# A head's keys in one DMA with runs of 64 KB, into two overlapping homes in turn: cached attention with a dense block, one core

## The chip, the cores and the metric

The kernel runs on one core of one Trainium2 chip. The metric is the device time of one execution in microseconds. Of the version before there are three runs: 1279.92 us in the median, 1279.47 the lowest and 1280.14 the highest. A profiled execution of the same kernel stands beside them, and the rows in this document come from its trace.

## What is computed

One token passes through a layer: layer norm, attention of 32 heads over a cache of 32768 keys and values per head, output projection, and a dense block with the Mish activation. Everything is bf16. Cut to what matters:

```python
H, Sk, Dh, D, F = 32, 32768, 128, 512, 1376
q = (layernorm(x) @ wq).reshape(1, 1, H, Dh)            # one query per head
scores = einsum("bhqd,bhkd->bhqk", q, k_cache) * Dh ** -0.5
o = einsum("bhqk,bhkd->bhqd", softmax(scores), v_cache)
h = x + o.reshape(1, 1, H * Dh) @ wo
a = layernorm(h) @ w1 + b1
out = h + (a * tanh(softplus(a))) @ w2
```

k_cache and v_cache hold 8 MiB per head each, 512 MiB in all; every byte of them is read once. The weights come to about 11.2 MB.

## The kernel before, in words

**Tiling.** A head's 32768 keys lie as 128 partitions of 256 rows, 128 numbers each (SCOLS = 256). A tile is 128 keys by 128 numbers: row r of every partition. The 256 tiles of a head go through TensorE in 32 groups of GT = 8.

**Storage.** One array in SBUF, `ring`, has six slots of 32 KB per partition (L214). Slots 0 and 1 are the home of the two halves of a head's keys, slots 2 and 3 of its values, slot 4 of wq and later of w1 and w2, slot 5 of wo (HOMES, L284). There is one home for keys and one for values, so the DMA of the next head's half waits until this head's half has been used (`freed_by`, L295).

**Queues.** All big DMAs are started by SP, in the order written at L279 to L282: wq; then for each head the first half of the keys, the second half, the values; then wo in three pieces, w1, w2 in two. SP takes them one after the other: before each it waits for what frees the place, then starts it (L330 to L355). A key DMA moves a run of 32 KB per partition, a value DMA one of 64 KB; the values of the last head come in two halves.

**The loop.** The 32 heads are a hardware loop on TensorE, VectorE and ScalarE (`rounds`, L86, and `one`, L504). The loop's counter is in a register of each engine; waits inside the loop compare a semaphore with a multiple of the counter (L84). The order on each engine is fixed when the program is written. A round does the following.

1. `k_group` (L442), 32 times: TensorE transposes 8 key tiles into one of four PSUM banks (L452); the first transpose of each half waits for that half's DMA. VectorE copies the bank to SBUF as bf16 (L455). Three groups later TensorE multiplies the 8 transposed tiles with the query, one column of scores each (`scores`, L429). The last transpose of a half frees the half's home.
2. `soft_max`, `soft_a`, `soft_b` (L477 to L491): the maximum over all scores, by VectorE over columns, TensorE over partitions, and back.
3. `soft_exp` (L493): ScalarE computes the exponential of all 256 columns in one instruction, which also sums them, and writes `pbuf`.
4. `pv` (L462): 256 products of a value tile with its column of `pbuf` (L466). The first waits for the exponential and for the values' DMA; the last frees the values' home. After 64 of them comes the sum over partitions (`soft_c`, L498), whose reciprocal VectorE takes (L501).
5. `oev` (L472): VectorE scales the result and puts it into column h of `oT`, at an address held in a register (L473).

**Around the loop.** Ahead of it are the layer norm and the 32 queries (L405). Behind it are the output projection (L538), the second layer norm and the dense block (L555 to L577), whose result goes out by a DMA from SP (L356). GpSimd has small work at the start: identity patterns, and 31 memsets of one number which only raise the semaphore of the last head's second half of values, so that the loop's waits hold in every round (L367).

Of the kernel before, what the change touches and what calls it, by code (L numbers as in the profile page):

```python
# [168 lines left out]
def build_kernel(nc, A_x, A_k_cache, A_v_cache, A_wq, A_wo, B_w1, B_b1, B_w2, out):  # L169
# [27 lines left out]
    assert W1 + (FJ + 1) * D <= SLOT  # L197
# [16 lines left out]
    ring = sb([128, NS, SLOT], BF16, "ring")  # L214
# [6 lines left out]
    esum = sb([128, 1], F32, "esum")  # L221
# [3 lines left out]
    skip = sb([1, H], F32, "skip")  # L225
# [17 lines left out]
    outr = sb([128, 128], BF16, "outr")  # L243
# [9 lines left out]
    C_REG = hlp[:, 129:130]  # L253
# [9 lines left out]
    kinds = [PE, ACT, DVE, POOL, SP, "exp", "pmax", "gmax", "qc", "A", "B", "C", "pv", "nb", "rcp"]  # L263
    kinds += [f"{k}{i}" for i in range(2 * GPS) for k in ("ev", "tr", "qk")]
    sems = {k: sem(f"s_{k}") for k in kinds}
    ready = [sem(f"ready{i}") for i in range(NS)]
# [17 lines left out]
    HOMES = {"k": 0, "v": HALVES, "wq": 2 * HALVES, "w1": 2 * HALVES, "w2": 2 * HALVES, "wo": 2 * HALVES + 1}  # L284

    def slot_of(what):
        return HOMES[what[0]] + (what[2] if what[0] == "k" else 0)

    def ready_wait(what):
        return (ready[slot_of(what)], 16 * (what[1] + 1 if what[0] in "kv" else 1))  # L290

    def free_name(what):
        return "free" + "_".join(map(str, what))

    def freed_by(what):  # L295
        if what[0] in ("w1", "w2"):
            return [free_name(WQ)]
# [4 lines left out]
    def flat_of(what):  # L302
        if what[0] == "v":
            return ring[:, HALVES:2 * HALVES, :].rearrange("p s x -> p (s x)")
        return ring[:, slot_of(what), :]

    def tiles_of(what):
        return flat_of(what).rearrange("p (r d) -> p r d", d=Dh)

    wq_v = ring[:, slot_of(("wq",)), :].rearrange("p (k n) -> p k n", k=KC)  # L310
    wo_f = ring[:, slot_of(("wo",)), :]
    wo_v = wo_f.rearrange("p (j n) -> p j n", j=32)
    w12 = ring[:, slot_of(("w1",)), :]
    w1_v = w12[:, 0:W1].rearrange("p (k n) -> p k n", k=KC)
    w2_v = w12[:, W1:W1 + (FJ + 1) * D].rearrange("p (j n) -> p j n", j=FJ + 1)

    events = {}

    def program(S):
# [10 lines left out]
        for what in order:  # L330
            slot = slot_of(what)
            S.wait(SP, freed_by(what))
            flat = flat_of(what)
            if what[0] == "wq":
                start(wq_v, A_wq.rearrange("(k p) n -> p k n", k=KC), ready[slot])
            elif what[0] == "wo":
                j0, j1 = WO_J[what[1]:what[1] + 2]
                start(wo_f[:, j0 * D:j1 * D], A_wo.rearrange("(p j) n -> p (j n)", j=32)[:, j0 * D:j1 * D], s_wo[what[1]])
            elif what[0] == "w1":
                start(w1_v, B_w1.rearrange("(k p) n -> p k n", k=KC), s_w1)  # L340
            elif what[0] == "w2":
                j0, j1 = W2_J[what[1]:what[1] + 2]
                if j0 < FJ:
                    start(w2_v[:, j0:j1, :], B_w2[j0 * 128:j1 * 128, :].rearrange("(j p) n -> p j n", p=128), s_w2[what[1]])
                else:
                    start(w2_v[0:FLAST, FJ, :], B_w2[FJ * 128:F, :], s_w2[what[1]])
            else:
                cache = A_k_cache if what[0] == "k" else A_v_cache
                rows = cache[0, what[1], :, :].rearrange("(p r) d -> p (r d)", r=SCOLS)
                at = what[2] * SLOT if what[0] == "k" else 0  # L350
                if what == ("v", H - 1):
                    start(flat[:, 0:SLOT], rows[:, 0:SLOT], ready[slot])
                    start(flat[:, SLOT:], rows[:, SLOT:], s_half)
                else:
                    start(flat, rows[:, at:at + flat.shape[-1]], ready[slot])  # L355
# [16 lines left out]
        S.dma(POOL, lambda: g.dma_start(b1r[FJ:FJ + 1, 0:FLAST], B_b1[FJ * 128:F].rearrange("(o p) -> o p", o=1)).then_inc(s_b1, 16))  # L372
        S.step(DVE, lambda: v.memset(oT[:, :], 0.0), name="oTz")
# [27 lines left out]
        for h in range(H):  # L401
            for kc in range(KC):
                last = h == H - 1 and kc == KC - 1
                bg = kc - NE if h == H - 1 else None
                S.step(PE, lambda h=h, kc=kc: t_.matmul(Q_REG[:, h:h + 1], wq_v[:, kc, h * Dh:(h + 1) * Dh],  # L405
                                                         xnT[:, 0, kc:kc + 1], start=(kc == 0), stop=(kc == KC - 1)),
                       name=([f"qkb{bg}"] + (["q", free_name(WQ)] if last else []) if bg is not None else None),
                       kind=(f"qk{bg % (2 * GPS)}" if bg is not None else None),
                       waits=(["xn0", ready_wait(("wq",))] if h == 0 and kc == 0 else ()))
# [27 lines left out]
        def k_group(h, half, gi):  # L437
            what = ("k", h, half)
            bg = count[0]
            count[0] += 1  # L440
            kt = tiles_of(what)
            tb = T_b[bg % NT]  # L442
            for r in range(GT):
                waits = []
                if r == 0:
                    if gi == 0:
                        waits.append(ready_wait(what))
# [4 lines left out]
                S.step(PE, lambda r=r: t_.matmul(tb[:, r * 128:(r + 1) * 128], kt[:, gi * GT + r, :], identb[:, :],  # L452
# [5 lines left out]
            pend.append((h, half * TPS + gi * GT, bg))  # L458
# [3 lines left out]
        def pv(h, r0, r1):  # L462
            vt = tiles_of(("v", h))
            for r in range(r0, r1):
                last = r == SCOLS - 1
                S.step(PE, lambda r=r, last=last: t_.matmul(o_ps[:, 0:1], vt[:, r, :], pbuf[:, r:r + 1],  # L466
                                                            start=(r == 0), stop=last),
                       name=([free_name(("v", h)), f"pv{h}"] if last else None), kind=("pv" if last else None),
                       waits=([f"exp{h}", ready_wait(("v", h))] if r == 0 else
# [23 lines left out]
        def soft_exp(h):  # L493
            S.step(ACT, lambda: a.activation(pbuf[:, :], S_ps[:, 0:SCOLS], ACTF.Exp,  # L494
                                             bias=nb[:, :], scale=SC, accum_out=esum[:, :]),
                   name=f"exp{h}", waits=[f"nb{h}"], kind="exp")

        def soft_c(h):  # L498
            S.step(PE, lambda: t_.matmul(C_REG, onesm[:, :], esum[:, :], start=True, stop=True),  # L499
                   name=f"C{h}", waits=[f"exp{h}"], kind="C")  # L500
            S.step(DVE, lambda: v.reciprocal(rtotc[:, :], C_REG), name=f"rcp{h}",  # L501
                   waits=[f"C{h}"], kind="rcp")

        def one(n):  # L504
            h = n - 1
            for half in range(HALVES):
                for gi in range(GPS):
                    k_group(h, half, gi)
# [112 lines left out]
```

## Time and profile before

| what | value |
|---|---|
| median of three runs | 1279.92 us |
| the profiled execution's own time | 1279.57 us |
| its span, first to last instruction | 1277.8 us |
| DMA read from HBM | 548.08 MB |
| mean rate over the span | 429 GB/s |
| mean granted TensorE clock | 0.768 of full |
| TensorE's matmuls, number | 25131 |

How to read it: the difference between the execution's time and its span lies before the first and after the last instruction. In the profile PE is TensorE's matmuls, PEld its weight loads (they overlap), DVE is VectorE, ACT ScalarE, POOL GpSimd, SP SyncE; a letter q behind an engine marks an instruction that its sequencer handles, such as a register operation or the start of a DMA. A row of the timeline has start, length, engine, line, operation and tiles, the number of equal instructions merged in it, and in brackets the idle time of the engine ahead of it with what ended it. The chain of waits is followed back from the last instruction, at each step to what released it. A view of one line gives the shortest, median and longest duration in ns, and the first and last start in us.

### The profile page before, as it was taken

Reading aid. Unit: us, or ns where it says so; the run is one execution under the profiler, and the core shown is the slowest. Engines: PE = TensorE matmul, PEld = TensorE weight load, DVE = VectorE, ACT = ScalarE, POOL = GpSimd, SP = SyncE. Lnnn points to the kernel's source line nnn. Section 1 sums busy time; section 2 is a strip of 40 time slices with the busy share of each in tenths; the row PEclk is TensorE's granted clock in tenths of the full one; section 3 lists DMA queues with packets and bytes.
Section 4 is the critical chain, followed back from the end, with each engine's and each line's share of the span. In section 5 each row is a group of like instructions: output and inputs, shape, how many; then the busy total and the mean of one; then the engine's idle time right before and its main releaser. Section 6 shows DMA issues by size and latency. Waiting matters only on the chain.

```text
span 1277.8 us, 53266 instructions
## 1 busy us (share of the span) xinstructions
PE 1013.8 (79%) x25131; PEld 992.0 (78%) x25131; DVE 715.1 (56%) x1247; ACT 20.6 (2%) x70; POOL 3.3 (0%) x40
## 2 busy tenths in 40 slices
PE   3789877879777889777888778797778797778886
PEld 3789877878777878777888778787778797778885
DVE  2566544566444666445665445664446664456652
ACT  0000000000000000000000000000000000000000
POOL 1000000000000000000000000000000000000000
PEclk9788776888677887767887768886778877678875
DMA  9999999999999999999999999999999999999998
GB/s 407 426 425 436 443 427 421 439 428 446 433 431 425 432 430 449 427 423 436 429 444 435 429 426 432 429 451 427 431 427 430 429 450 427 427 432 430 451 418 328
DMA packets 16955, 548.25 MB, mean 429 GB/s; under 512 B 1744, under 2 KB 3120, under 8 KB 3760
## 3 DMA queue, kind: packets, MB, share of 16 engines
q1 hardware_dynamic: 16872, 548.09, 99.6%
q8 instruction: 9, 0.15, 0.0%
q0 software_dynamic: 64, 0.00, 0.0%
q14 instruction: 2, 0.02, 0.0%
q10 hardware_dynamic: 8, 0.00, 0.0%
HBM read 548.08 MB, written 0.00 MB: 429 GB/s over the span
## 4 chain that ended last, share of the span: by engine, by line
DMA 76%; PE 22%; issue 1%; DVE 0%; SPq 0%; ACT 0%; ACTq 0%
DMA ring<-in_A_v_cache_dram 71%; PE ops L466 17%; DMA ring<-in_B_w_dram 4%; PE tps L452 3%; DMA ring<-in_A_k_cache_dram 2%; PE hlp L499 1%; PE sps L429 1%; SPq L328 0%; DVE ering L455 0%; PE tps L571 0%; PE hlp L484 0%; PE hlp L489 0%; DVE pmax L478 0%; DVE gmax L486 0%; ACT pbuf L494 0%
## 5 line engine op out<-in xcount | busy, mean ns | idle before, releaser
L455 DVE COPY ering<-tps 128x1024 bf16<-128x1024 bf16 x1024 | 669.6, 692 | 125.3 <-PE tps L452 124.6
L452 PE MATMUL tps<-identb,ring 128*128 128x128 bf16 x8192 | 670.8, 233 | 74.5 <-DMA ring<-in_A_k_cache_dram 72.0
L452 PEld LDWEIGHTS tps<-identb,ring 128*128 128x128 bf16 x8192 | 524.1, 104 | 77.3 <-DMA ring<-in_A_k_cache_dram 74.5
L429 PE MATMUL sps<-qcur,ering 128*128 128x1 bf16 x8192 | 343.9, 164 | 8.7 <-DVE ering L455 6.7
L466 PEld LDWEIGHTS ops<-pbuf,ring 128*128 128x128 bf16 x8192 | 229.7, 105 | 132.1 <-issue 129.3
L466 PE MATMUL ops<-pbuf,ring 128*128 128x1 bf16 x8192 | 227.7, 165 | 130.1 <-DMA ring<-in_A_v_cache_dram 123.6
L429 PEld LDWEIGHTS sps<-qcur,ering 128*128 128x128 bf16 x8192 | 310.4, 97 | 11.6 <-DVE ering L455 9.4
L501 DVE RECIPROCAL rtotc<-hlp 128x1 f32<-128x1 f32 x32 | 5.4, 168 | 193.9 <-PE hlp L499 193.9
L473 DVE TENSOR_TENSOR oT<-ops,rtotc 128x1 f32 x32 | 5.2, 161 | 166.2 <-PE ops L466 166.2
L494 ACT ACTIVATE pbuf<-sps,nbias 128x256 bf16<-128x256 f32 x32 | 15.2, 474 | 1229.5 <-DVE nbias L491 1229.5
L489 PEld LDWEIGHTS hlp<-gmax,onesmat 1*128 1x128 f32 x64 | 11.7, 227 | 21.6 <-DVE gmax L486 21.6
L484 PE MATMUL hlp<-ident,pmax 128*1 128x128 f32 x64 | 12.4, 276 | 16.6 <-DVE pmax L478 16.6
L489 PE MATMUL hlp<-gmax,onesmat 1*128 1x1 f32 x64 | 14.4, 292 | 11.9 <-DVE gmax L486 11.9
L478 DVE TENSOR_REDUCE pmax<-sps 128x1 f32<-128x256 f32 x32 | 13.6, 424 | 16.5 <-PE sps L429 16.5
L499 PE MATMUL hlp<-esum,onesmat 128*128 128x1 f32 x64 | 18.1, 352 | 0.0
L484 PEld LDWEIGHTS hlp<-ident,pmax 128*1 128x1 f32 x64 | 2.7, 81 | 19.4 <-DVE pmax L478 19.4
L486 DVE TENSOR_REDUCE gmax<-hlp 1x1 f32<-1x128 f32 x32 | 8.9, 279 | 13.4 <-PE hlp L484 13.4
L499 PEld LDWEIGHTS hlp<-esum,onesmat 128*128 128x128 f32 x64 | 16.1, 312 | 0.0
L491 DVE TENSOR_SCALAR nbias<-hlp 128x1 f32<-128x1 f32 x32 | 5.0, 158 | 17.4 <-PE hlp L489 17.4
L405 PE MATMUL hlp<-xnT,ring 128*128 128x1 bf16 x128 | 3.6, 165 | 9.7 <-DMA ring<-in_A_wq_dram 9.7
L405 PEld LDWEIGHTS hlp<-xnT,ring 128*128 128x128 bf16 x128 | 3.5, 104 | 9.8 <-issue 9.8
L411 DVE CAST qT<-hlp 128x32 bf16<-128x32 f32 x1 | 0.2, 191 | 12.0 <-PE hlp L405 12.0
(59 smaller groups left out, 39.6 us busy)
## 6 DMA issues: line engine op xcount, KB each, us to landing
ring<-in_A_k_cache_dram SPq DMA_DIRECT2D x64, 4096.0 KB, 26.7
ring<-in_A_v_cache_dram SPq DMA_DIRECT2D x2, 4096.0 KB, 26.3
ring<-in_A_wq_dram SPq DMA_DIRECT2D x1, 4096.0 KB, 12.5
ring<-in_A_wo_dram SPq DMA_DIRECT2D x1, 2048.0 KB, 35.3
ring<-in_A_wo_dram SPq DMA_DIRECT2D x1, 1536.0 KB, 38.6
ring<-in_B_w_dram SPq DMA_DIRECT2D x1, 1376.0 KB, 42.4
ring<-in_B_w_dram SPq DMA_DIRECT2D x1, 1280.0 KB, 46.8
ring<-in_A_wo_dram SPq DMA_DIRECT2D x1, 512.0 KB, 39.4
```

The lines of the kernel that those rows point to most:

```text
L405: S.step(PE, lambda h=h, kc=kc: t_.matmul(Q_REG[:, h:h + 1], wq_v[:, kc, h * Dh:(h + 1) * Dh], xnT[:, 0, kc:kc + 1], start=(kc == 0), stop ...
L429: S.step(PE, lambda r=r: t_.matmul(S_ps[:, col0 + r:col0 + r + 1], ering[:, bg % NE, r, :], qcur[:, :], start=True, stop=True), name=(name ...
L452: S.step(PE, lambda r=r: t_.matmul(tb[:, r * 128:(r + 1) * 128], kt[:, gi * GT + r, :], identb[:, :], is_transpose=True, start=True, stop= ...
L455: S.step(DVE, lambda: v.tensor_copy(ering[:, bg % NE, :, :].rearrange("p r d -> p (r d)"), tb[:, :]), name=f"ev{bg}", waits=[f"trb{bg}", f ...
L466: S.step(PE, lambda r=r, last=last: t_.matmul(o_ps[:, 0:1], vt[:, r, :], pbuf[:, r:r + 1], start=(r == 0), stop=last), name=([free_name((" ...
L478: S.step(DVE, lambda: v.tensor_reduce(pmax[:, :], S_ps[:, 0:SCOLS], AXX, ALU.max), name=f"pmax{h}", waits=[f"qkh{h}"], kind="pmax")
L484: S.step(PE, lambda: t_.matmul(A_REG, pmax[:, :], ident[:, :], start=True, stop=True), name=f"A{h}", waits=[f"pmax{h}", "ident"], kind="A")
L486: S.step(DVE, lambda: v.tensor_reduce(gmax[:, :], A_REG, AXX, ALU.max), name=f"gmax{h}", waits=[f"A{h}"], kind="gmax")
L489: S.step(PE, lambda: t_.matmul(B_REG, onesm[0:1, :], gmax[:, :], start=True, stop=True), name=f"B{h}", waits=[f"gmax{h}", "consts0"], kind ...
L494: S.step(ACT, lambda: a.activation(pbuf[:, :], S_ps[:, 0:SCOLS], ACTF.Exp, bias=nb[:, :], scale=SC, accum_out=esum[:, :]), name=f"exp{h}", ...
L499: S.step(PE, lambda: t_.matmul(C_REG, onesm[:, :], esum[:, :], start=True, stop=True), name=f"C{h}", waits=[f"exp{h}"], kind="C")
L501: S.step(DVE, lambda: v.reciprocal(rtotc[:, :], C_REG), name=f"rcp{h}", waits=[f"C{h}"], kind="rcp")
```

## The change

A head's keys come in one DMA, as its values do, with a run of 64 KB per partition. Two whole homes for keys don't fit, so two homes overlap: keys take 256 + 80 tiles' room, heads with an even number use the first 256, heads with an odd number the last 256. The 176 tiles in the middle belong to both homes; their place doesn't depend on the head. They are transposed first, as score columns 0 to 175. The other 80 lie in front of the middle for even heads and behind it for odd ones; they come as columns 176 to 255, and their address is computed from the loop's counter (`S.base`).

The next head's DMA is started when the last of the 176 tiles has been transposed (`free_k`). The score columns no longer stand in the order of the rows, so the exponential is done in two instructions, one per part, each written to the place in `pbuf` where the values' order wants it (a register address, too), and their two sums are added by one more instruction of VectorE (`etot`). In the instruction order of the changed kernel a fused register operation stands in front of each of the 80 transposes in TensorE's loop, and one in front of each exponential on ScalarE.

Heads 0, 30 and 31 get their keys in three DMAs, of 88, 88 and 80 columns. TensorE waits for each of the three parts in every round; for the heads between, 58 memsets of GpSimd, which wait for the first head's parts, raise the semaphores of parts 1 and 2. w1 gets a home of its own, w2 goes into the first 80 tiles of the keys' room, wo into wq's home. The output row uses part of `ering`.

The core of the diff:

```diff
+    DYN = 80
+    FIX = SCOLS - DYN
+    CUT = [0, FIX // 2, FIX, SCOLS]
+    KB, VB, WA, WB_ = (SCOLS + DYN) * Dh, SCOLS * Dh, SLOT, W1 + 640
...
+    PARTS = [0, H - 2, H - 1]
+    def parts(h):
+        return range(3) if h in PARTS else (None,)
     for h in range(H):
-        order += [("k", h, half) for half in range(HALVES)] + [("v", h)]
+        order += [("k", h, part) for part in parts(h)] + [("v", h)]
...
+        if what[0] == "wo":
+            return ["free_wq"]
+        if what[0] == "w2":
+            return [f"free_d{H - 2}"]
+        if what[0] == "k" and what[2] == 2 and what[1] > 0:
+            return [f"free_d{what[1] - 1}"]
         if what[0] in "kv" and what[1] > 0:
-            return [free_name((what[0], what[1] - 1) + what[2:])]
+            return [f"free_{what[0]}{what[1] - 1}"]
...
+    def base(h):
+        return DYN * (h % 2)
...
+                if what[0] == "k" and what[2] is None:
+                    start(k_f[:, base(h) * Dh:(base(h) + SCOLS) * Dh], rows, ready["k0"])
+                elif what[0] == "k":
+                    c0, c1 = CUT[what[2]:what[2] + 2]
+                    t0 = DYN + c0 if c0 < FIX else (base(h) + FIX if h % 2 else 0)
+                    t1 = t0 + c1 - c0
+                    start(k_f[:, t0 * Dh:t1 * Dh], rows[:, (t0 - base(h)) * Dh:(t1 - base(h)) * Dh], ready[f"k{what[2]}"])
...
+        S.wait(POOL, [(ready["k1"], 16), (ready["k2"], 16)])
+            for n in range(H - len(PARTS)):
+                g.memset(skip[:, H + n:H + n + 1], 0.0).then_inc(ready["k1"], 16)
+                g.memset(skip[:, 2 * H + n:2 * H + n + 1], 0.0).then_inc(ready["k2"], 16)
...
+            def tile(c):
+                if c < FIX:
+                    return k_t[:, DYN + c, :]
+                if c == FIX:
+                    S.base = nc.snap(((S.counter + 1) % 2) * (SCOLS * Dh), engines=[LOOPED[PE]], min_val=0, max_val=SCOLS * Dh)
+                return k_f[:, bass.ds(S.base + (c - FIX) * Dh, Dh)]
...
-                    names = [f"trb{bg}"] + ([free_name(what)] if gi == GPS - 1 else [])
-                S.step(PE, lambda r=r: t_.matmul(tb[:, r * 128:(r + 1) * 128], kt[:, gi * GT + r, :], identb[:, :],
+                    names = [f"trb{bg}"] + ([f"free_k{h}"] if col0 + GT == FIX else [f"free_d{h}"] if col0 + GT == SCOLS else [])
+                S.step(PE, lambda r=r: t_.matmul(tb[:, r * 128:(r + 1) * 128], tile(col0 + r), identb[:, :],
...
-            S.step(ACT, lambda: a.activation(pbuf[:, :], S_ps[:, 0:SCOLS], ACTF.Exp,
-                                             bias=nb[:, :], scale=SC, accum_out=esum[:, :]),
-                   name=f"exp{h}", waits=[f"nb{h}"], kind="exp")
+            def part(n, c0, c1, at):
+                return lambda: a.activation(pbuf[:, bass.ds(at(S.counter), c1 - c0)], S_ps[:, c0:c1], ACTF.Exp,
+                                            bias=nb[:, :], scale=SC, accum_out=esum[:, n:n + 1])
+            S.step(ACT, part(0, 0, FIX, lambda i: (i % 2) * DYN), name=f"expa{h}", waits=[f"nb{h}"], kind="expa")
+            S.step(ACT, part(1, FIX, SCOLS, lambda i: ((i + 1) % 2) * FIX), name=f"exp{h}", waits=[f"nb{h}"], kind="exp")
...
+            S.step(DVE, lambda: v.tensor_reduce(etot[:, :], C_REG, AXX, ALU.add), name=f"etot{h}", waits=[f"C{h}"], kind="etot")
```

More of the change, by code (lines that the diff above doesn't have):

```diff
@@ L242, in build_kernel @@
     actT = sb([128, FJ + 1], BF16, "actT")
[L243 removed]
+    outr = ering[:, 0, 0, :]
     S_ps = ps([128, 512], "sps")
@@ L262, in build_kernel @@
     sem = nc.alloc_semaphore
-    kinds = [PE, ACT, DVE, POOL, SP, "exp", "pmax", "gmax", "qc", "A", "B", "C", "pv", "nb", "rcp"]
+    kinds = [PE, ACT, DVE, POOL, SP, "exp", "pmax", "gmax", "qc", "A", "B", "C", "pv", "nb", "rcp", "expa", "etot"]
     kinds += [f"{k}{i}" for i in range(2 * GPS) for k in ("ev", "tr", "qk")]
     sems = {k: sem(f"s_{k}") for k in kinds}
-    ready = [sem(f"ready{i}") for i in range(NS)]
+    ready = {k: sem(f"ready_{k}") for k in ("wq", "v", "k0", "k1", "k2")}
     s_x = sem("s_x")
```

94 lines of the change are left out of this document (40 added, 54 removed).

## The prediction

> **What bounds the kernel now.** I read the page first: engine shares, DMA rows, chain.
>
> ```profile
> span 1277.8 us, 53266 instructions
> PE 1013.8 (79%) x25131; PEld 992.0 (78%) x25131; DVE 715.1 (56%) x1247; ACT 20.6 (2%) x70; POOL 3.3 (0%) x40
> DMA  9999999999999999999999999999999999999998
> q1 hardware_dynamic: 16872, 548.09, 99.6%
> DMA 76%; PE 22%; issue 1%; DVE 0%; SPq 0%; ACT 0%; ACTq 0%
> ```
>
> The one hardware queue, which SP fills, keeps the 16 DMA engines busy for 99.6% of the span; TensorE is busy for 79%. Then the chain of waits in order of time, and the timeline of one head:
>
> ```profile
> 409.98 31.22 DMA ring<-in_A_v_cache_dram
> 441.34 1.84 PE ops L466 x64
> 448.76 31.23 DMA ring<-in_A_v_cache_dram
> ```
>
> ```profile
> 409.98 0.33 SPq L328 DMA_DIRECT2D ring<-in_A_v_cache_dram  x1
> 412.19 3.47 PE L452 MATMUL tps<-identb,ring 128*128 128x128 bf16 x32 [2.24 <-DMA ring<-in_A_k_cache_dram]
> 414.97 19.52 DVE L455 COPY ering<-tps 128x1024 bf16<-128x1024 bf16 x30 [0.16 <-PE tps L452]
> 415.50 0.34 PE L429 MATMUL sps<-qcur,ering 128*128 128x1 bf16 x8
> 416.32 0.45 PEld L452 LDWEIGHTS tps<-identb,ring 128*128 128x128 bf16 x8
> 423.45 10.67 SPq L328 DMA_DIRECT2D ring<-in_A_k_cache_dram  x2
> 436.98 0.47 ACT L494 ACTIVATE pbuf<-sps,nbias 128x256 bf16<-128x256 f32 x1 [37.92 <-DVE nbias L491]
> 437.35 0.19 ACT L494 ACTIVATION_READ_ACCUMULATOR pbuf<-sps,nbias 128x1 f32 x1
> 441.34 1.84 PE L466 MATMUL ops<-pbuf,ring 128*128 128x1 bf16 x64 [4.59 <-DMA ring<-in_A_v_cache_dram]
> 448.76 0.33 SPq L328 DMA_DIRECT2D ring<-in_A_v_cache_dram  x1
> 448.88 0.16 DVE L473 TENSOR_TENSOR oT<-ops,rtotc 128x1 f32 x1 [5.06 <-PE ops L466]
> 450.97 3.59 PE L452 MATMUL tps<-identb,ring 128*128 128x128 bf16 x32 [2.24 <-DMA ring<-in_A_k_cache_dram]
> ```
>
> The reader is to see a regular beat. Values are issued at 409.98 and 448.76: one head takes **38.78 us**. TensorE stands still twice in it, 4.59 us until the values land and 2.24 us until the next keys do, so the transfers set the beat. The chain's 31 us per value load are mostly queueing: the load was issued 11 us before the stream came to it. Landings of one head: first half of the keys at 412.1 (TensorE starts at 412.19), second about 9.7 us later (4.19 MB at the stream's 430 GB/s; 421.9), values at 441.2 (409.98 + 31.22).
>
> **The change, part by part.** Its own sum stands against the profiled execution: 1279.57 us, of which 1277.8 are the span and 1.8 lie around it; the median of the runs is 1279.92, 0.35 above. I add differences to the median.
>
> *Runs of 64 KB for keys.* The values already have them, so the trace prices them. Two DMA windows, the first nearly all values, the second nearly all keys:
>
> ```profile
> DMA packets 151, 8.09 MB, mean 418 GB/s; under 512 B 16, under 2 KB 16, under 8 KB 16
> q1 hardware_dynamic: 151, 8.09, 96.7%
> ...
> DMA packets 281, 8.68 MB, mean 446 GB/s; under 512 B 32, under 2 KB 32, under 8 KB 32
> q1 hardware_dynamic: 281, 8.68, 103.7%
> ```
>
> The windows are 19.35 and 19.45 us long. Bytes by busy time: 8.09 / (19.35 x 0.967) = 432.4 GB/s with 64 KB, 8.68 / (19.45 x 1.037) = 430.3 with 32 KB. A head's 8.39 MB of keys goes from 19.50 to 19.40 us: 0.095 us, and 29 heads (1 to 29) make 2.7 us. Heads 0, 30 and 31 come in three pieces of some 20 KB, 24 packets per engine instead of 16; at the same 0.095 us per 8 packets that gives back 0.3. The gain at most: **about 2.4 us** (1 to 3, as the rounded shares allow), if the stream stays unbroken. SP issues 29 key DMAs fewer at 0.33 us each; SP is idle most of the time, so nothing.
>
> *Keys in one piece: TensorE starts later.* Now a head's first transpose waits at 412.2 for half of the keys; afterwards it waits for all, at 421.9 in the same beat. The values land at 441.2 as before, so the 9.7 us come out of the slack behind. This is the heart of the sum, and I check both loads that wait on TensorE.
>
> (a) The next keys are issued after 176 tiles, 22 groups of 8. The groups' pace is 19.52 / 30 = 0.65 us; 16 groups ended at 423.45, 11.26 us after their start; 22 take 11.26 + 6 x 0.65 = 15.2. From 421.9 that is 437.1, while the values stream until 441.2. From issue to first bytes the start of the program shows:
>
> ```profile
> 0.75 0.46 SPq L328 DMA_DIRECT2D ring<-in_A_wq_dram  x1
> ...
> GB/s 0 0 0 0 0 0 0 0 0 0 0 0 0 0 0 0 0 0 0 0 0 0 7 7 0 765 546 437 0 0 0 0 0 0 109 109 0 109 437 655
> ```
>
> The slices of this window are 0.075 us: the bulk begins in the 26th, at 1.88, so 1.13 us after the issue. 437.1 + 1.1 = 438.2 is 3 us early. No stall.
>
> (b) The next values are issued when the products with the old ones end. In before they ended at 448.7, with 11 us to spare. Now: 421.9, plus key phase and softmax (412.19 to 437.55 and 0.1 to the first product: 25.45), plus 7.42 for the products (441.34 to 448.76), gives 454.8; plus 1.13 is 455.9, against 460.7 when the stream has ended the next keys (421.9 + 38.78). **Slack 4.8 us before anything is added to the phase.**
>
> *Register addresses: 80 per head, in the phase that has the slack.* The instruction order of the changed kernel has one fused register operation (three steps: add, multiply, add) in front of each of the 80 transposes, 10 groups. Before has one such operation per round on TensorE and two on VectorE:
>
> ```profile
> L91 PEldq FUSED_REGOPS  x32: 35/35/35, 21.0 to 1224.1; - x32
> L91 PEldq COMPARE_BRANCH  x33: 76/208/4558, 16.4 to 1259.2; - x33
> L84 PEldq EVENT_SEMAPHORE  x64: 51/51/51, 25.7 to 1251.1; - x64
> L84 DVEq EVENT_SEMAPHORE  x1056: 21/21/21, 17.4 to 1254.8; - x176
> L473 DVEq FUSED_REGOPS  x32: 57/57/71, 68.6 to 1259.8; - x32
> ```
>
> No row shows a register-addressed weight load. Lower bound: 35 ns, below the 56 ns that a transpose takes anyway (0.45 us for 8), nothing added. Upper bound: a sequencer operation as dear as the branch, 208 ns per tile. Nearest row: on VectorE the fused operation and its register-addressed instruction together. SP and VectorE were released by the same event; SP's DMA started at 448.76, L473's instruction at 448.88: 0.12 us for the pair. TensorE's sequencer spends 51 ns on a semaphore operation where VectorE's spends 21, so I add 0.03: **0.15 us per tile**. The 8 scores of a group (0.34 us with the pipeline's tail, 0.2 of issue: 0.65 - 0.45) are static and I set them behind: 8 x 0.15 + 0.2 = 1.40 instead of 0.65, 0.75 more; 10 groups: **X = 7.5 us per head**, between 0 and (8 x 0.208 + 0.2 - 0.65) x 10 = 12.
>
> The Trainium skill's TensorE: Matmul & The Clock Gate ("Wait — 56ns, not 53.3ns?") says that matmuls and weight loads normally go past the sequencer's microcode and that through it one costs about 62 ns; the 56 ns above agree with the first. An estimate by that page: 35 + 62 = 97 ns per tile, X = 3.3, no loss. No run here shows which way a register-addressed load takes.
>
> *Exponential in two.* One activation and one read of the sum (0.47 + 0.19) become two of each. Between 0.2 and 0.66 us more ahead of the products; two short ones overlap in part: 0.4. The added reduce on VectorE lies beside the three quarters of the products that follow. Nothing.
>
> *What else moves.* 58 GpSimd memsets wait for the first head's keys; nothing is queued behind them, and head 1's groups need them a beat later. Two more waits per head on TensorE for semaphores long reached: nothing (51 ns each if the cover is gone). Output and MLP weights have other homes, the same bytes and order. Nothing.
>
> *Sum.* First the clock, in rows by stretch (length; busy time of PE, PEld, DVE, ACT, POOL; granted clock; DMA share, GB/s): products, first 32 transposes, rest of the key phase.
>
> ```profile
> 402.50:409.90 7.40, 7.34 (x258) 7.34 (x258) 0.17 (x1) 0.00 (x0) 0.00 (x0) 0.50 0.99 425
> 412.19:415.44 3.25, 3.25 (x32) 3.25 (x32) 1.85 (x3) 0.00 (x0) 0.00 (x0) 0.51 1.08 464
> 415.44:437.60 22.16, 20.22 (x488) 19.66 (x485) 19.94 (x34) 0.56 (x2) 0.00 (x0) 0.96 1.02 439
> ```
>
> The first 32 transposes run at half clock (0.51) after the idle times. If TensorE hardly idles they take 4 x 0.45 = 1.8 instead of 3.25: 1.45 us back. The same page ("What's actually happening") puts the drop to half clock after about 3.4 us without work; the idle times of 4.59 and 2.24 and the 0.50 are in line with that.
>
> Keys landing, TensorE's turn, issue of the next values, their transfer and that of the keys behind them, landing: this ring goes around once in **two** heads, since the keys between are already on their way. Twice the beat = 0.05 + (25.45 - 1.45 + 0.4 + X) + 7.42 + 1.13 + 2 x 19.35 = 71.7 + X. It binds when it is over 2 x 38.7: at **X = 5.7**, that is 0.13 us per tile (4.3 with the cold start). TensorE alone needs 25.45 - 1.45 + 0.4 + 7.42 = 31.8, plus X, per head. At X = 7.5: ring 79.2 / 2 = 39.6, TensorE 39.3. The beat goes from 38.78 to 39.6; 29 heads x 0.82 = 23.8 us: 1279.9 + 23.8 = **1303.7 us**.
>
> **Rivals.**
>
> *The stream still hides it (the other side).* Below 0.13 us per tile X stays under 5.7, the values are issued in time, and only the shorter transfers are left: 1279.9 - 2.4 = 1277.5. For: 35 ns is the only TensorE row of such an operation, and the 16 static score instructions of a group may run beside the next address. Against: 0.12 us for the pair on VectorE, and TensorE's other sequencer operations of 51 ns and more.
>
> *TensorE becomes the bound.* Above 0.18 us per tile (X over 10) its 31.8 + X exceeds the ring: 41.8 at X = 10, 29 x 3.0 = 88 us, 1367; at 0.208 (X = 12) 1425. For: the branch row, and that a load with its address in a register may not be queued ahead. Against: the 35 ns.
>
> *Half clock.* Should the gaps between register-addressed tiles bring the clock back to 0.50, the 1.45 us return: ring (73.2 + 7.5) / 2 = 40.3, 1325. Inside the forecast's range.
>
> *The keys' issue comes late.* It has 3 us; TensorE would have to be 3 us slower before tile 176, where nothing is added. Left out.
>
> **How the numbers follow.** Forecast (0.13 to 0.18 us per tile, 1281 to 1365): 0.44. Hidden by the stream: 0.42; its gain of 1 to 3 us lies around the 2.6 us that are 0.2%, about what a measurement of this kernel can tell from no change, so 0.08 of it is faster and 0.34 no difference. TensorE as the bound, over 1365: 0.14. No difference in all, with the lowest edge of the forecast: 0.36; slower 0.56. The range takes in the hidden case and the forecast: 1276.5 to 1365. The likeliest case's own range is 1281 to 1365.
>
> **What would show it.** Right: the DMA row well below 99.6%; value loads issued after the keys before them have landed; in the chain, TensorE's transposes at the register-addressed line with a share like the value loads'; the DVE copies of the last 10 groups some 1.4 us apart, the first 22 at 0.65; no wait for values ahead of L484's products. Wrong: the copies stay under 1.2 us apart, TensorE still waits for keys by more than 1 us in each head, the beat stays at 38.7. The packets' rate would show 432 GB/s for keys in either case, and a lower rate would break the first term.

## The result and the profile after

The changed kernel takes **1326.15 us** (median of six runs, 1322.51 to 1328.13), against 1279.88 for the kernel before, measured beside it. The ratio is 1.0358 (95% interval 1.034 to 1.0375): 46.3 us slower. The profiled execution is the quickest of the six, 1322.51 us with a span of 1320.7, so what the trace shows is 42.9 us of span; the medians lie 3.4 us further apart.

The page of the changed kernel: span, engines (busy us, share, instructions), the hardware queue (packets, MB, share of the 16 DMA engines), shares of the chain.

```profile
span 1320.7 us, 56019 instructions
PE 1125.9 (85%) x25131; PEld 1052.0 (80%) x25131; DVE 734.0 (56%) x1279; ACT 28.3 (2%) x134; POOL 5.3 (0%) x98
q1 hardware_dynamic: 13128, 548.08, 97.9%
DMA 56%; PE 43%; DVE 1%; issue 1%; ACT 0%; ACTq 0%; SPq 0%; DVEq 0%
```

The bytes are the same, but the queue is busy for 97.9% of a longer span, and TensorE holds 43% of the chain, twice its share before. Neither is the bound alone. The chain in order of time (start, length, who) shows what they do together:

```profile
566.92 24.10 DMA ring<-in_A_k_cache_dram
591.07 3.43 PE tps L471 x32
...
606.16 25.31 DMA ring<-in_A_k_cache_dram
631.52 3.60 PE tps L471 x32
...
646.80 24.61 DMA ring<-in_A_k_cache_dram
671.46 3.59 PE tps L471 x32
```

TensorE now waits for every head's keys, and the beat (from one head to the next) is about 40 us (591.07, 631.52, 671.46). The timeline of one head in between (start, length, engine, what, and in brackets the idle time ahead of it and who ended it):

```profile
606.16 0.33 SPq L330 DMA_DIRECT2D ring<-in_A_k_cache_dram  x1
607.93 0.69 DVE L474 COPY ering<-tps 128x1024 bf16<-128x1024 bf16 x1 [0.35 <-PE tps L471]
608.98 0.69 DVE L474 COPY ering<-tps 128x1024 bf16<-128x1024 bf16 x1 [0.35 <-PE tps L471]
610.04 0.69 DVE L474 COPY ering<-tps 128x1024 bf16<-128x1024 bf16 x1 [0.37 <-PE tps L471]
619.62 0.41 ACT L513 ACTIVATE pbuf<-sps,nbias 128x176 f32 x1 [38.79 <-DVE nbias L509]
620.02 0.32 ACT L513 ACTIVATE pbuf<-sps,nbias 128x80 f32 x1
620.23 0.20 ACT L513 ACTIVATION_READ_ACCUMULATOR pbuf<-sps,nbias 128x1 f32 x1
620.53 1.85 PE L484 MATMUL ops<-pbuf,ring 128*128 128x1 bf16 x64 [1.28 <-ACT pbuf L513]
627.96 0.33 SPq L330 DMA_DIRECT2D ring<-in_A_v_cache_dram  x1
631.52 3.60 PE L471 MATMUL tps<-identb,ring 128*128 128x128 bf16 x32 [3.59 <-DMA ring<-in_A_k_cache_dram]
646.80 0.33 SPq L330 DMA_DIRECT2D ring<-in_A_k_cache_dram  x1
```

Three things are to be seen. The copies of register-addressed groups stand 1.05 us apart, not 0.65 and not the forecast's 1.4. The products at 620.53 wait for the exponential and no longer for values. And the values are issued at 627.96, when the keys ahead of them in the queue are nearly in: these land at 631.47 on the slowest of the 16 DMA engines (606.16 + 25.31). The stream breaks there. Three stretches (length; busy time of PE, PEld, DVE, ACT, POOL; granted clock; DMA share, GB/s): first transposes, products, and what follows the value issue:

```profile
591.07:594.65 3.58, 3.58 (x43) 3.58 (x44) 2.19 (x4) 0.00 (x0) 0.00 (x0) 0.57 0.74 311
620.50:627.95 7.45, 7.39 (x258) 7.34 (x258) 0.32 (x2) 0.00 (x0) 0.00 (x0) 0.50 0.98 422
627.95:631.50 3.55, 0.00 (x0) 0.00 (x0) 0.16 (x1) 0.00 (x0) 0.00 (x0) 0.50 0.79 295
```

295 GB/s in 3.55 us, where 430 would be the stream's pace, is 1.1 us of transfer missing in this head. The clock column says that the first transposes are still slow (0.57), and that the products run at half clock too (0.50).

How early a load joins the queue can be read from the list of DMA issues (number, median us from issue to landing). The transfer alone takes 19.4 us; the rest of the time is what the load was issued ahead plus what it lost.

```profile
ring<-in_A_v_cache_dram SPq DMA_DIRECT2D x31, 23.9
ring<-in_A_k_cache_dram SPq DMA_DIRECT2D x29, 24.4
```

4.5 us for values, where before had 11.8 (31.2 - 19.4).

To separate the two parts I took each load's last packet on each of the 16 engines. **Lead** is the mean landing of the load ahead less the issue; **loss** is the time between the two mean landings less 19.36 us, the unbroken transfer. Over heads issued between 100 and 1180 us (some 27 loads of each kind): values lead by 1.55 us and lose 1.15 each (31.1 in all), keys lead by 3.5 and lose 0.19 (5.2 in all). In before values lead by 11.2 and lose 0.00. Two heads are then 4 x 19.36 + 2 x (1.15 + 0.19) = 80.1 us, a beat of 40.05; the value issues from 110.59 to 1190.88, 27 beats, give 40.01.

So of the span's 42.9 us, 34.3 arise between the landings of the values of heads 2 and 29, 1.8 ahead of them, 2.7 in heads 30 and 31, and 4.1 behind the last weight DMA (its mean landing lies 5.4 us before the end in before, 9.5 us now).

### The profile page after: what moved, and what is told of

Its sections match the earlier page's. It is cut to its first block, busy times and chain, and to the rows that moved or that the text cites. A ratio compares the mean times of both kernels' runs of the same rounds, so it can differ in the third digit from the quotient of the medians.

```text
span 1320.7 us, 56019 instructions
## 1 busy us (share of the span) xinstructions
PE 1125.9 (85%) x25131; PEld 1052.0 (80%) x25131; DVE 734.0 (56%) x1279; ACT 28.3 (2%) x134; POOL 5.3 (0%) x98
## 3 DMA queue, kind: packets, MB, share of 16 engines
q1 hardware_dynamic: 13128, 548.08, 97.9%
## 4 chain that ended last, share of the span: by engine, by line
DMA 56%; PE 43%; DVE 1%; issue 1%; ACT 0%; ACTq 0%; SPq 0%; DVEq 0%
DMA ring<-in_A_k_cache_dram 56%; PE tps L471 32%; PE sps L441 8%; PE ops L484 2%; PE yps L558 0%; DVE ering L474 0%; PE hlp L507 0%; PE sps L575 0%; PE tps L591 0%; PE hlp L502 0%; DVE pmax L496 0%; PE hlp L519 0%; ACT pbuf L513 0%; DVE gmax L504 0%; PE hlp L401 0%
## 5 line engine op out<-in xcount | busy, mean ns | idle before, releaser
L471 PE MATMUL tps<-identb,ring 128*128 128x128 bf16 x8192 | 782.4, 234 | 96.3 <-DMA ring<-in_A_k_cache_dram 94.3
L474 DVE COPY ering<-tps 128x1024 bf16<-128x1024 bf16 x1024 | 683.5, 691 | 245.1 <-PE tps L471 243.7
L471 PEld LDWEIGHTS tps<-identb,ring 128*128 128x128 bf16 (+1 forms) x8192 | 595.3, 104 | 151.2 <-DMA ring<-in_A_k_cache_dram 96.8
L521 DVE TENSOR_REDUCE etot<-hlp 128x1 f32<-128x2 f32 x32 | 5.1, 159 | 108.5 <-PE hlp L519 108.5
L513 ACT ACTIVATE pbuf<-sps,nbias 128x176 f32 x64 | 22.9, 363 | 1268.1 <-DVE nbias L509 1268.1
L507 PE MATMUL hlp<-gmax,onesmat 1*128 1x1 f32 x64 | 15.2, 305 | 11.8 <-DVE gmax L504 11.8
L496 DVE TENSOR_REDUCE pmax<-sps 128x1 f32<-128x256 f32 x32 | 13.6, 424 | 14.3 <-PE sps L441 14.3
L502 PEld LDWEIGHTS hlp<-ident,pmax 128*1 128x1 f32 x64 | 2.7, 80 | 19.4 <-DVE pmax L496 19.4
L519 PE MATMUL hlp<-esum,onesmat 128*128 128x2 f32 x64 | 18.1, 353 | 0.0
L513 ACT ACTIVATION_READ_ACCUMULATOR pbuf<-sps,nbias 128x1 f32 x64 | 12.5, 196 | 0.0
## 6 DMA issues: line engine op xcount, KB each, us to landing
ring<-in_A_wo_dram SPq DMA_DIRECT2D x1, 2048.0 KB, 31.2
```

Of the source, the lines that this page charges most:

```text
L474: S.step(DVE, lambda: v.tensor_copy(ering[:, bg % NE, :, :].rearrange("p r d -> p (r d)"), tb[:, :]), name=f"ev{bg}", waits=[f"trb{bg}", f ...
L496: S.step(DVE, lambda: v.tensor_reduce(pmax[:, :], S_ps[:, 0:SCOLS], AXX, ALU.max), name=f"pmax{h}", waits=[f"qkh{h}"], kind="pmax")
L502: S.step(PE, lambda: t_.matmul(A_REG, pmax[:, :], ident[:, :], start=True, stop=True), name=f"A{h}", waits=[f"pmax{h}", "ident"], kind="A")
L507: S.step(PE, lambda: t_.matmul(B_REG, onesm[0:1, :], gmax[:, :], start=True, stop=True), name=f"B{h}", waits=[f"gmax{h}", "consts0"], kind ...
L513: return lambda: a.activation(pbuf[:, bass.ds(at(S.counter), c1 - c0)], S_ps[:, c0:c1], ACTF.Exp, bias=nb[:, :], scale=SC, accum_out=esum[ ...
```

## Experiments

The theory after the result: SP can issue a load only when TensorE has freed its home; the register-addressed tiles make that late, and a load that is issued too shortly ahead of the end of the one before it breaks the stream. Rivals: registers cost TensorE the time by themselves; the one-piece keys cost it whatever the tiles do; the half-speed start costs it.

### e1: the 80 tiles at a fixed address

```diff
-                return k_f[:, bass.ds(S.base + (c - FIX) * Dh, Dh)]
+                return identb[:, :]
```

> The changed kernel, but the 80 tiles of columns 176 to 255 are a constant tile at a fixed address instead of the register-addressed keys (it leaves those keys out of the computation; all transfers and waits stay). In the profile after, a register-addressed group takes 1.045 us instead of 0.65, so 4.0 us per head go. Theory (late issue: keys' landing, TensorE's turn, issue of the values, and some 4.75 us more than the two transfers themselves until the next keys but one have landed, 80.4 us for two heads): 76.4 us for two heads, 38.2 each, below the stream's 38.7, so the stream is the bound again: 1277 to 1282 us, DMA row over 99%, value packets back at one beat of 19.35 us. Rival (the transfers themselves are slower with 64 KB key runs into changing homes: packets of 64 KB took 2469 ns on average instead of 2423, 22 us in all): those 22 us stay, 1300 us or more.

Measured: 1293.67 us, ratio 1.0102 (1.0087 to 1.0118). Missed: by difference the registers' part is 32.5 us, but 13.9 us stay without any. The issues and one passage (timeline) of this kernel, whose profiled execution is the longest of its four (1296.71 us):

```profile
ring<-in_A_v_cache_dram SPq DMA_DIRECT2D x31, 25.0
ring<-in_A_k_cache_dram SPq DMA_DIRECT2D x29, 23.6
```

```profile
659.90 0.33 SPq L330 DMA_DIRECT2D ring<-in_A_v_cache_dram  x1
665.36 3.27 PE L469 MATMUL tps<-identb,ring 128*128 128x128 bf16 x32 [5.49 <-DMA ring<-in_A_k_cache_dram]
680.30 0.33 SPq L330 DMA_DIRECT2D ring<-in_A_k_cache_dram  x1
```

Values are issued 5.5 us before TensorE gets the keys and lose 0.08 us each. Now the keys are the late ones: 23.6 - 19.4 = 4.2 us of lead and loss together; by the landings they lead by 2.4 and lose 0.57 each, 15.5 in all. Their issue needs 176 tiles, 14.9 us after TensorE's start (680.30 - 665.36). That is close to the prediction's 15.2; what was wrong was to call the 3 us that remain enough.

### e2: registers in the kernel before

Tiles 176 to 255 of each head stay in before's homes, but are addressed by a register; so that the address depends on the counter, every other head takes them one tile earlier:

```diff
+            def tile(c):
+                if c < SCOLS - 80:
+                    return kt[:, c - half * TPS, :]
+                if c == SCOLS - 80:
+                    S.base = nc.snap(((S.counter + 1) % 2) * Dh + (SCOLS - 81) * Dh, ...)
+                return flat[:, bass.ds(S.base + (c - (SCOLS - 80)) * Dh, Dh)]
```

> The kernel before with one part of the change alone: the transposes of columns 176 to 255 get their address from a register, in the same two homes (heads with an odd number take their keys one tile earlier there, so one tile is counted twice and the last left out). Theory: the phase grows by the same 4.0 us, the values are issued 4 us later, 7 us ahead of the stream instead of 11, so nothing is lost: 1279 to 1282 us with groups of 1.04 us. Rival (the register operations cost by themselves, TensorE's time is the bound): 4 us per head less whatever idle time is left cannot be hidden, 1300 us or more.

Measured: 1280.32 us, ratio 1.0005 (0.9996 to 1.0014). No loss, as expected. The timeline of one head:

```profile
429.49 0.69 DVE L464 COPY ering<-tps 128x1024 bf16<-128x1024 bf16 x1 [0.33 <-PE tps L461]
430.51 0.69 DVE L464 COPY ering<-tps 128x1024 bf16<-128x1024 bf16 x1 [0.33 <-PE tps L461]
441.40 1.87 PE L475 MATMUL ops<-pbuf,ring 128*128 128x1 bf16 x64 [0.85 <-ACT pbuf L503]
448.84 0.33 SPq L328 DMA_DIRECT2D ring<-in_A_v_cache_dram  x1
```

Groups 1.02 us apart: the price per tile is the same as in the changed kernel, and all of it falls into the 4.59 us for which TensorE waited for values before. So the values' issue does not come 4 us later, as was expected, but at the old place (448.84, in before 448.76). Registers by themselves cost this kernel nothing that these runs can tell.

### e3: values in two DMAs, the first half's home freed after 128 products

```diff
-                    start(v_f, rows, ready["v"])
+                    a0 = what[2] * SLOT
+                    start(v_f[:, a0:a0 + SLOT], rows[:, a0:a0 + SLOT], s_half if what[2] else ready["v"])
```

(with a wait and a semaphore of its own for each half)

> The changed kernel, but every head's values come in two DMAs of 32 KB runs, and the first half's home is freed after 128 of the 256 products. The first half is issued about 3.7 us earlier. Theory (late issue): 80.4 - 3.7 = 76.7 us for two heads, the stream is the bound again; the values' runs of 32 KB cost what the keys' runs gained, 0.095 us per head: 1279 to 1284 us. Rival (slower transfers of the keys): the keys' packets stay slow, 1305 us or more.

Measured: 1300.51 us, ratio 1.0169 (1.0155 to 1.0183). Missed: 25.6 us come back, 20.8 stay. The issues:

```profile
ring<-in_A_k_cache_dram SPq DMA_DIRECT2D x29, 23.5
ring<-in_A_v_cache_dram SPq DMA_DIRECT2D x64, 4096.0 KB, 20.8
```

The values' part of the theory holds: their first halves lead by 4.1 us and lose 0.06 each. The keys, which led by 3.5 us while values stalled the stream, lead by 2.5 now and lose 0.34 (9.1 in all); and the end lies 11.8 us behind the last weight DMA instead of 9.5. As in e1, the second load in line takes over.

### e4: 32 transposes of a constant after the products

They are meant to bring the clock up in the time in which TensorE waits for keys.

```diff
             pv(h, 64, SCOLS)
+            for r in range(32):
+                S.step(PE, lambda: t_.matmul(y_warm, identb[:, :], identb[:, :], is_transpose=True, start=True, stop=True))
```

> The changed kernel plus 32 transposes of a constant after a head's products, while TensorE waits 3.6 us for the next keys; nothing reads them. At half clock they take 3.4 us. Theory: the clock is up when the keys land, the first 32 transposes take 1.8 instead of 3.4 to 3.6 us; 1.5 us less on the ring of two heads, 0.75 per head, 29 heads: about 1305 us. Rival (the half clock is not what holds the ring, or the extra work runs into the keys' landing): 1326 us or more.

Measured: 1319.61 us, ratio 1.0319 (1.0304 to 1.0335), 6.5 us better than the change where some 21 were expected. One head:

```profile
661.96 3.57 PE L539 MATMUL yps<-identb 128*128 128x128 bf16 x32
662.12 0.33 SPq L331 DMA_DIRECT2D ring<-in_A_v_cache_dram  x1
665.58 3.02 PE L472 MATMUL tps<-identb,ring 128*128 128x128 bf16 x32
```

Here the 32 constant tiles take 3.57 us at half speed, and the 32 real ones behind them still 3.02. But this head is one of the slower ones. Over the 27 heads that start between 100 and 1180 us the first 32 transposes take 2.47 us in the mean (1.95 to 3.59) where the change has 3.55, and the 176 that free the keys' home take 14.13 where it has 15.54. So the clock did come up, and on average it gave the 1.4 us that were expected of it.

The beat got only part of them. In 8 of 26 heads the constant tiles were still running when the keys had landed, and held the real ones back by 0.2 to 1.2 us. And a part goes into the lead: values lead by 2.2 us instead of 1.55 and lose 0.73 instead of 1.15, keys lead by 4.3 instead of 3.5. The expectation had counted the whole gain as time off the ring. Last, the end lies 15.7 us behind the last weight DMA, 6 more than in the change: 3.6 of these are the last head's own constant tiles, which stand ahead of the output projection with nothing to wait for.

### e5 and e6: the kernel before, with its value issue held back

Here nothing of the change is in the kernel; only SP waits for a later point of TensorE's key phase before it issues the values: for group 10 (e5) or group 4 (e6).

```diff
             S.wait(SP, freed_by(what))
+            if what[0] == "v" and what[1] > 0:
+                S.wait(SP, [f"trb{2 * GPS * what[1] + 9}"])
```

(+ 3 instead of + 9 in e6)

> The kernel before, unchanged on every engine but SP: a head's values (from head 1 on) are issued only when TensorE has transposed the tenth group of that head's keys, some 10 us later than before, 1 to 2 us ahead of the stream instead of 11. Nothing else of the change is in it: no register address, no 64 KB run for keys. Theory (lateness alone): the changed kernel's loads with such a lead landed 1.1 us later than one transfer after the load ahead of them, mean over the 16 engines; 31 heads, 34 us: 1305 to 1320 us, with 64 KB packets over 2.42 us on average. Rival (1.1 us from the issue to the first bytes is all that a load needs, as the prediction had it; the overlapping homes or the 64 KB key runs are what slows the transfers): 1279 to 1285 us.

> The same with the fourth group instead of the tenth: the values are issued some 4 us earlier than in the run with the tenth, 5 to 6 us ahead of the stream. Theory (a lead of 4 to 5 us suffices): 1279 to 1282 us. Rival (any wait of this kind costs, or the lead has to be more): 1285 us or more.

Measured: e5 1339.92 us, ratio 1.0485 (1.0467 to 1.0503), more than expected, since the lead came out at 0.7 us and not at 1 to 2; e6 1281.96 us, ratio 1.0016 (1.0007 to 1.0025), as expected. SP's value issues in e5, then the median time from issue to landing in e5 and in e6:

```profile
437.83 0.33 SPq L328 DMA_DIRECT2D ring<-in_A_v_cache_dram  x1
478.57 0.33 SPq L328 DMA_DIRECT2D ring<-in_A_v_cache_dram  x1
518.47 0.33 SPq L328 DMA_DIRECT2D ring<-in_A_v_cache_dram  x1
```

```profile
ring<-in_A_v_cache_dram SPq DMA_DIRECT2D x31, 23.0
```

```profile
ring<-in_A_v_cache_dram SPq DMA_DIRECT2D x31, 25.4
```

Same instructions, same bytes, same packets; only the issue is later. With a lead of 4.5 us (e6) nothing is lost, with 0.7 us (e5) 1.73 us per load, 46.7 over the 27 issued between 100 and 1180 us, and these two beats are (518.47 - 437.83) / 2 = 40.3 us. What e6 has over before, 2.2 us, goes with a single load: head 1's values were issued 0.4 us ahead and lost 1.8. This is the direct proof that a late issue alone makes such a loss, with no register and no one-piece keys.

It also answers the rival of e1, that 64 KB key runs into changing homes are what slows the transfers. The 64 KB packets take 2423 ns in the mean in before, 2469 in the change, but 2506 in e5, which has neither; in e7 below, which has the homes and no late issue, 2423.

### e7: the change with every head's keys in three DMAs

```diff
-    PARTS = [0, H - 2, H - 1]
+    PARTS = list(range(H))
```

> The changed kernel, but every head's keys come in three DMAs of 88, 88 and 80 tiles, as those of heads 0, 30 and 31 do; overlapping homes, register addresses and the split exponential stay. TensorE starts some 13 us earlier in the beat, both issues get that much more lead. Theory (the start after the whole landing is what makes both issues late): 24 packets per engine instead of 16 cost 0.095 us per head, 3 us: 1281 to 1286 us. Rival (register addresses or the homes slow it): 1300 us or more.

Measured: 1282.17 us, ratio 1.0019 (1.001 to 1.0028), as expected. The line group of the products (count, busy us, mean ns, idle ahead and who ended it), then the issues:

```profile
L484 PE MATMUL ops<-pbuf,ring 128*128 128x1 bf16 x8192 | 227.5, 165 | 93.3 <-DMA ring<-in_A_v_cache_dram 84.3
```

```profile
ring<-in_A_v_cache_dram SPq DMA_DIRECT2D x31, 31.3
```

All the rest of the change is still there: registers, overlapping homes, the exponential in two. But TensorE starts on a third of the keys, values have their 11.0 us of lead again, and the products wait for them (84.3 us in all) as they did before. Its 2.41 us over before go with 8 more packets per engine in 32 heads, so one piece instead of two should be worth about as much the other way; no run measures that alone.

### e8: fixed addresses and 48 transposes of a constant

e1's edit, and behind the products:

```diff
             pv(h, 64, SCOLS)
+            for r in range(48):
+                S.step(PE, lambda: t_.matmul(y_warm, identb[:, :], identb[:, :], is_transpose=True, start=True, stop=True))
```

> The changed kernel with the constant tiles at a fixed address (the last 80 columns' keys are left out) and 48 transposes of a constant while TensorE waits 5.5 us for the next keys. With the constant tiles alone it took 1293.7 us; its key loads were issued 1.8 us ahead of the first engine's end and landed 0.57 us late on average, 15.5 us over 27 heads; its value loads 3.7 us ahead, 2 us in all. Theory (the keys' issue is what is late there): the clock is up sooner, the first 176 tiles take 1.0 to 1.5 us less, the key loads have 3 us of lead and lose 0.15 to 0.25: 1281 to 1286 us. Rival (what is left there is not the keys' issue but the homes or the split exponential): 1291 us or more.

Measured: 1283.89 us, ratio 1.0042 (1.002 to 1.0064), as expected. Issues, then one passage of the timeline:

```profile
ring<-in_A_v_cache_dram SPq DMA_DIRECT2D x31, 26.2
ring<-in_A_k_cache_dram SPq DMA_DIRECT2D x29, 25.0
```

```profile
649.35 5.28 PE L537 MATMUL yps<-identb 128*128 128x128 bf16 x48
649.52 0.33 SPq L331 DMA_DIRECT2D ring<-in_A_v_cache_dram  x1
656.67 1.96 PE L470 MATMUL tps<-identb,ring 128*128 128x128 bf16 x32 [2.04 <-DMA ring<-in_A_k_cache_dram]
```

The first 32 transposes take 1.96 us here instead of e1's 3.27. Over all heads it is 2.46 us in the mean instead of 3.53, and 14.3 instead of 15.6 for the 176, so the keys' home is free 1.3 us sooner. Keys lead by 4.2 us and lose 0.10, values by 5.7 and lose 0.00: 1.8 us more of lead took away four fifths of e1's loss on keys. What is left over before, 4.1 us, is at the end, which lies 10.0 us behind the last weight DMA instead of 5.4. There the last head's own constant tiles hold up the output projection:

```profile
1264.59 5.12 PE L537 MATMUL yps<-identb 128*128 128x128 bf16 x48
```

Between the landings of the values of heads 2 and 29 this kernel is 1.0 us behind before. So overlapping homes and the split exponential cost next to nothing in the loop once both loads have over 4 us of lead.

## Why the prediction was right in its sign and its case, and where its terms failed

**What held.** TensorE waits only for keys; the values come late; the ring through TensorE's turn and two transfers sets the beat; the stream is no longer full. The forecast's case came, and 1326 lies in its range, 22 us above the predicted time.

Not all of its own signs came, though. Two of the three that were to show it wrong did: the copies stand 1.05 us apart, under 1.2, and TensorE still waits for keys, 3.59 us in the head above; only the third, a beat that stays at 38.7, did not. And the value loads are not issued after the keys have landed, but ahead of it (627.96, the first engine's landing is at 629.42).

**But the way there was not the one written down.** The measured ring, from rows shown above: keys landing 591.02, TensorE's turn of 36.9 us to the value issue at 627.96, and 43.5 us from there to the landing of the keys after next at 671.41 (646.80 + 24.61).

| term, two heads | predicted, us | measured, us |
|---|---|---|
| register-addressed groups, X | 7.5 | 10 x (1.05 - 0.65) = 4.0 |
| half-speed start of the transposes | 1.45 taken off | not taken off |
| TensorE's turn in all | 39.4 | 36.9 |
| from the value issue, beyond the two transfers | 1.13 | 43.5 - 38.7 = 4.75 |
| ring | 79.2 | 80.4 |

*X was too large.* The 0.15 us per tile had been taken from VectorE's pair of operations. The trace has TensorE's own row, in the view of line L471 (duration in ns: least, median, most):

```profile
L471 PEldq FUSED_REGOPS  x2528: 46/46/46, 40.4 to 1294.3; - x195
```

A group of eight takes 0.40 us more, not 0.75. The 35 ns row of TensorE's own sequencer was the nearer one. The Trainium skill's figure, from which the prediction had X = 3.3 (TensorE: Matmul & The Clock Gate, "Wait — 56ns, not 53.3ns?"), comes nearer than its own 7.5; how such a load is issued no run here shows.

*The clock did not come back.* TensorE idles 3.59 us ahead of the keys, and the next 32 transposes take 3.60 us; in the mean 3.55, as in e7, and 3.54 in before. So the half-speed start is no part of what the change costs: before has it too. That it stays was a rival ("half clock"), for another reason, gaps between tiles. What the prediction had wrong is what halves the clock. It took the idle times for the cause. But in the head above the clock falls at 618.07, 1.9 us after the last transpose, and stays at 0.50 all through the products, while the 3.59 us without work begin only at 627.93; the prediction's own row of the products shows 0.50 as well. The Trainium skill's rule (TensorE: Matmul & The Clock Gate, "What's actually happening": half speed after about 3.4 us without work) does not describe this drop, if work means TensorE's busy time.

*The lead was the step that failed.* A group of 1.05 us is 0.106 us per tile by the prediction's formula (8 x 0.106 + 0.2), below the 0.13 from which it let the ring bind. With X = 4.0 and the cold start, its own ring is 73.2 + 4.0 = 77.2, below 2 x 38.7: by its sum the stream would have hidden the change, 1277.5 us. It didn't, because 1.13 us from issue to first bytes, read at the start of the program with an empty queue, is not the lead that keeps a running queue full. A load issued 1.55 us ahead of the mean end lost 1.15 us; e5 shows the same with nothing else changed. So that the beat of 39.6 stands close to the measured 40.0 is luck: TensorE's turn was put 2.5 us too long (X too high by 3.5, less the cold start that was wrongly taken off), the time behind the issue 3.6 too short, and the two nearly cancel.

*A slip in the sums.* By the prediction's own terms TensorE's 31.8 + X passes the ring's (71.7 + X) / 2 at X = 8.1, 0.16 us per tile, and not at 10. At the X = 7.5 that it used the ring is still the longer one, so the predicted time is unchanged.

*Step (a) fails for the same reason.* "3 us early. No stall": the issue came at the place that was forecast, and the lead of 2.4 us that e1 measures costs 0.57 us in each head, 13.9 us in all with nothing else in the way. The rival that I left out was real.

*What held in size.* The exponential in two: 619.62 to the second read's end at 620.43 is 0.81 us, where before had 0.56; 0.25 more, within the bounds and below the 0.4 taken. The longer runs: e7 pays 2.4 us for three pieces instead of two, which fits the 2.4 predicted for one instead of two; in the change this is buried.

*From 23.8 to 46.3 us.* The beat's 0.4 us more over 29 heads makes 11.6. Heads 30 and 31 and the end add 6.8, for which the prediction had no term, and the median lies 3.4 further from before's than the profiled spans do; 0.7 is left over. In the end part TensorE is behind the last weight DMA: the final product of before (first row) waits for the DMA, that of the changed kernel (second row) for VectorE.

```profile
1274.00 1.34 PE L571 MATMUL tps<-ring,actT 128*1 128x128 bf16 x44 [3.36 <-DMA ring<-in_B_w_dram]
1316.93 1.34 PE L591 MATMUL tps<-ring,actT 128*1 128x128 bf16 x44 [1.59 <-DVE actT L586]
```

**The whole in one line:** registers alone cost nothing (e2), nor do registers with keys in parts (e7); keys in one piece alone cost 13.9 us (e1); both together 46.3. The change spends the values' 11 us of lead on TensorE's late start, and the registers then take the rest of it.

## What to carry to other kernels

Where a queue of transfers is the bound, write down for each load how long before the end of the one ahead it can be issued, and look at that slack, not at the wait that is to be removed. Longer runs per packet were worth some 2 us here and could not pay for it. A load in one piece puts off the first work by its whole transfer, and so everything that this work sets free. Keep several us of lead: the loads here lost next to nothing when they were issued over 4 us before the mean landing of the load ahead. And read a clock or a wait over many heads before taking one row for the rule: the head shown for e4 was one of its slow ones.

## What the runs showed of the hardware

*Loads on one queue lost time unless they were issued over 4 us ahead.* Mean loss of an 8.4 MB load by its lead, from the landings between 100 and 1180 us in all kernels of this study:

| lead, us | loss per load, us |
|---|---|
| 0 to 0.5 | 2.1 |
| 0.5 to 1 | 1.5 |
| 1 to 2 | 1.15 |
| 2 to 2.5 | 0.7 |
| 2.5 to 3 | 0.23 |
| 3 to 4 | 0.13 |
| over 4 | 0.00 |

The single loads scatter widely around these means (0.0 to 1.9 us at a lead of 2 to 2.5). The loss goes along with 16 engines that don't end together. In the change's head above, 15 of them had moved the last of the keys by 629.8 and one at 631.2. The values' first packets began between 629.1, which is 1.14 us after the issue, and 631.6: on average 0.48 us after the engines' last packets of keys. And the first two packets took 2.81 us each in the mean instead of 2.42. Together that is 1.26 us. So the 1.13 us from issue to first bytes do hold, but only for the first engine. Over the whole run the queue is busy for about 1293 us (97.9% of 1320.7) instead of 1273: slower packets make about half of the 42.9 us, idle engines the rest. Which of the queue's steps takes the time was not tried.

*The transposes wake the clock, the products don't.* The products keep TensorE busy for 7.39 of 7.45 us at a clock of 0.50. In the change's trace the clock steps at 594.18 (up), 618.07 (down), 635.14 (up), 659.03 (down) and 676.10 (up): 7, 5, 7 and 5 times 3.41 us apart. How soon a row of transposes gets the full clock thus depends on where it lies between these steps. In the head shown of e4 the transposes behind 3.57 us of constant ones took 3.02 us, in that of e8, behind 5.28 us of them and 2.04 us of waiting, 1.96; over all heads the means are 2.47 and 2.46, so 48 constant tiles did no more for the clock than 32.

*Register addresses on TensorE cost 46 ns of sequencer time each, and 0.05 us per tile in a stream of transposes and scores.*
